# Memory reads of four units as sixteen 32x32 tiles, with new engine orders, in a gated attention and token-mixing kernel

## The chip, the core and the metric

The kernel runs on one core of one Trainium2 chip. The metric is device time in microseconds, the median of several executions. The core has a matmul engine (PE, with its weight loads shown as PEld), a vector engine (DVE), an activation engine (ACT), a general engine (POOL) and a queue engine (SP) that here issues nearly all DMAs. Matmuls write PSUM, which is split into eight banks; a bank holds 512 fp32 values in each of 128 partitions. DVE and ACT read PSUM; everything else lives in SBUF.

## What is computed

The reference mixes two branches with a gate per token (S = 2048 tokens, D = 448):

```python
g = sigmoid((x * gate_w).sum(-1, keepdims=True))
a = A(x, wq, wk, wv, wo, beta)      # attention with a running memory
b = B(x, w1, b1, w2, b2)            # layer norm, then an MLP over the token axis
return g * a + (1 - g) * b
```

Branch A has H = 16 heads of 28 values. The tokens are cut into N = 4 segments of 512. Within a segment the attention is causal softmax attention; from earlier segments a head reads a memory:

```python
phi = lambda t: where(t > 0, t + 1, exp(t))
a_dot = softmax(qs @ ks.T * scale + mask) @ vs      # inside the segment
a_mem = (phi(qs) @ M) / (phi(qs) @ z + 1e-6)        # from earlier segments
o = sigmoid(beta) * a_mem + (1 - sigmoid(beta)) * a_dot
M = M + phi(ks).T @ vs;  z = z + phi(ks).sum(0)
```

The heads' outputs go through `wo`. Branch B is `gelu(h.T @ w1 + b1) @ w2 + b2` on the layer-normed tokens, transposed back; w1 is 2048 x 1792 and w2 is 1792 x 2048.

## The kernel before

**Units and names.** The heads lie in four groups of four, each head padded to 32 rows, so that a group fills 128 partitions. A unit u = 0 to 15 is one segment (u // 4) of one head group (u % 4). `sc{p}_{f}` fills the four score banks 0 to 3 with scores of a pair of units, five fills f for each pair p; ACT's `exp{p}_{f}` empties them (L951) and POOL masks the diagonal blocks (L954). `pv{u}` is the value product (L978), 16 matmuls in four column tiles; each value tile has a 29th column of ones, so the softmax denominator comes with it. `mst{s}` adds a segment's phi(k)v into the memory (L827), and `mstc{s}` (L845) writes it to SBUF as matmul weights. Before, the weights of a group are four 128-column blocks, one per head, each zero outside its head's rows: a 128x128 block-diagonal matrix. `mem{u}` is the memory read of unit u = 4 to 15: one 128x128 matmul on 512 columns of phi(q), into a bank that it takes from the pool of banks 4 to 7. DVE then transposes read and value product out of PSUM (`tm` L992, `ta` L994), adds 1e-6 (`eps` L1003), takes reciprocals (`rec`), scales (`oa`, `om`), adds both (`o`, on POOL or DVE) and transposes back (`ot` L1016). `wo{T}` multiplies token tile T by `wo`, and `ag{T}` applies the gate.

**MLP.** `u{ft}-{st}` are the 14 x 16 matmuls of w1 (448 columns each), followed by the gelu steps `gsq`, `gvh`, `garg`, `gth`, `gelu`. `y{T}-{ft}` are the 16 x 14 matmuls of w2; `fin{T}` (L1082) adds the gated attention and `out{T}` stores the tile. Tile 15 is cut in two parts of 320 and 128 columns; the second carries `#1`.

**Start.** `warm` runs nine matmuls on constants (L625). `dtx{t}_{k}` load x transposed, 512 tokens at a time, in parts of three and one 128-column chunks; `ldx{t}` load four token tiles of x for the layer norm; `ldwv`, `ldwk`, `ldwq` load weights in chunks. `gtr` and `btr` transpose the gate vector and the biases on PE, DVE's `gw`, `b1c`, `b2c` copy them out, and `padk`, `padx`, `padq` (L636) spread the key and query weights into padded heads. Projections are `pra`/`prb` (first chunks), `lo...` (pairs on half the array each, for the last chunk), and `prt` (values), `prk`, `prx`, `prq`. `bns`, `bna` (L885, L887) are the layer norm's statistics and `ln` applies them.

**Order.** Each engine runs a list written out by hand or planner in `ORDER`, in order; a word `name@b` takes PSUM bank b, `name*n` is n consecutive matmuls. Waits follow from the data. In `plan` PE's list is cut into runs between operations on row tiles or half-arrays (modes "r", "h"). Where such a run has a column-tiled operation (mode "c": `pv`, `mst`), all plain matmuls in it (mode "x") are issued as four column tiles too:

```python
for o in self.per_eng["PE"] + [None]:
    if o is None or o.tile != "f":
        for x in run:
            x.cols = x.mode == "x" and any(y.mode == "c" for y in run)
        run = []
```

Of the kernel before, what the change touches and what calls it, by code (L numbers as in the profile page):

```python
# [6 lines left out]
ALU = mybir.AluOpType  # L7
# [7 lines left out]
DH = 28  # L15
# [7 lines left out]
NHG = 4  # L23
# [51 lines left out]
class Sched:  # L75
# [13 lines left out]
    def op(self, eng, fn, reads=(), writes=(), name=None, dma=False, out=False, cost=100.0, prio=0.0, mode="f",  # L89
# [13 lines left out]
        o.tile = mode if mode in "rh" else "f"  # L103
# [196 lines left out]
pv5@5 u10-6*5 sc3_2 u10-11 u11-0@4 u10-12 u11-1 u10-13*3 mst1@5 u11-2*4 sc3_3 lot10@75 u11-6*3 prt11 u11-9 prt10  # L300
# [66 lines left out]
def build_kernel(nc, X, WQ, WK, WV, WO, BETA, W1, B1, W2, B2, GW, OUT):  # L367
# [842 lines left out]
```

## Time and profile before

| | us |
|---|---|
| median of 3 runs | 172.59 |
| lowest, highest | 172.51, 580.05 |
| span of the profiled execution | 170.6 |
| PE busy in it | 166.8 |
| DVE busy | 143.7 |
| ACT busy | 128.0 |
| POOL busy | 61.5 |

The span runs from the first to the last instruction of one execution. Of the three runs two lie within 0.1 us; the third is far off and is not used. Rows of the profile read as: line, engine, operation, tiles, shapes, count, then busy time, mean duration of one in ns, and the idle time just before with what ended it. Matmuls overlap in the pipeline, so the time from one start to the next tells more than a duration. The chain that ended last is followed back from the last instruction to what released each step; its rows are start, duration, engine, line, and how many instructions were merged.

### The profile page before, as it was taken

Reading aid. Unit: us, or ns where it says so; the run is one execution under the profiler, and the core shown is the slowest. Engines: PE = TensorE matmul, PEld = TensorE weight load, DVE = VectorE, ACT = ScalarE, POOL = GpSimd, SP = SyncE. Lnnn points to the kernel's source line nnn. Section 1 sums busy time; section 2 is a strip of 40 time slices with the busy share of each in tenths; the row PEclk is TensorE's granted clock in tenths of the full one; section 3 lists DMA queues with packets and bytes.
Section 4 is the critical chain, followed back from the end, with each engine's and each line's share of the span. In section 5 each row is a group of like instructions: output and inputs, shape, how many; then the busy total and the mean of one; then the engine's idle time right before and its main releaser. Section 6 shows DMA issues by size and latency. Waiting matters only on the chain.

```text
span 170.6 us, 5820 instructions
## 1 busy us (share of the span) xinstructions
PE 166.8 (98%) x2470; PEld 81.3 (48%) x2470; DVE 143.7 (84%) x327; ACT 128.0 (75%) x158; POOL 61.5 (36%) x94
## 2 busy tenths in 40 slices
PE   8899999999999999999999999999999999999994
PEld 2334444455444544545444345444454645555563
DVE  3088998858999899999999989999999999998024
ACT  0359997999999999989999999986897879002100
POOL 5000317255044333229465560446834372500000
DMA  6998994999796816234037286116146251553603
GB/s 145 252 280 274 238 219 138 290 256 183 173 235 168 142 33 184 38 94 138 4 115 207 65 257 112 33 32 187 46 143 200 83 156 50 156 161 112 188 4 108
DMA packets 52589, 25.16 MB, mean 148 GB/s; under 512 B 17092, under 2 KB 52324, under 8 KB 52564
## 3 DMA queue, kind: packets, MB, share of 16 engines
q1 hardware_dynamic: 51772, 24.22, 56.5%
q10 hardware_dynamic: 792, 0.58, 1.7%
q8 instruction: 19, 0.31, 0.8%
q14 instruction: 6, 0.05, 0.1%
HBM read 18.76 MB, written 2.36 MB: 124 GB/s over the span
## 4 chain that ended last, share of the span: by engine, by line
PE 93%; DMA 3%; SPq 2%; DVE 0%; issue 0%
PE t L264 80%; PE t L942 8%; PE t L978 5%; DMA t<-in_A_wk_dram 3%; SPq L521 2%; PE t L827 1%; DVE t L636 0%; DVE t L1082 0%; PE t L860 0%
## 5 line engine op out<-in xcount | busy, mean ns | idle before, releaser
L264 PE MATMUL t<-t 128*32 128x448 bf16 (+6 forms) x1753 | 145.2, 348 | 0.6 <-DMA t<-in_A_wv_dram 0.5
L264 PEld LDWEIGHTS t<-t 128*32 128x32 bf16 (+1 forms) x1753 | 66.8, 97 | 63.3 <-issue 12.8
L951 ACT ACTIVATE t<-t 128x2048 bf16<-128x2048 f32 x40 | 75.1, 1877 | 8.1 <-PE t L942 7.5
L954 POOL TENSOR_SCALAR_AFFINE_SELECT t<-t 128x512 bf16<-128x512 bf16 x64 | 43.4, 694 | 46.4 <-ACT t L951 45.4
L1009 POOL TENSOR_TENSOR t<-t 128x448 bf16<-128x448 f32 x9 | 11.3, 1254 | 18.9 <-DVE t L1007 9.2
L1082 DVE SCALAR_TENSOR_TENSOR t<-t 128x448 bf16<-128x448 f32 (+2 forms) x17 | 10.8, 643 | 8.6 <-PE t L264 8.1
L1036 ACT ACTIVATE t<-t 128x448 bf16<-128x448 f32 x10 | 7.2, 725 | 12.0 <-PE t L264 11.9
L942 PE MATMUL t<-t 28*128 28x512 bf16 (+3 forms) x256 | 15.8, 301 | 0.0
L994 DVE STREAM_TRANSPOSE t<-t 128x512 f32<-128x512 f32 x16 | 11.3, 709 | 1.2 <-PE t L978 0.8
L894 POOL TENSOR_TENSOR t<-t 128x4 f32<-128x4 f32 x4 | 4.3, 1069 | 21.4 <-DVE t L892 16.9
L978 PE MATMUL t<-t 128*32 128x512 bf16 (+3 forms) x256 | 11.5, 299 | 0.0
L942 PEld LDWEIGHTS t<-t 28*128 28x128 bf16 x256 | 4.4, 92 | 14.6 <-ACT t L951 5.9
L1016 DVE STREAM_TRANSPOSE t<-t 128x512 bf16<-128x512 bf16 x16 | 11.0, 689 | 0.1
L885 DVE BATCH_NORM_STATS2 t<-t 128x6 f32<-128x448 bf16 x16 | 9.2, 610 | 0.7 <-DMA t<-in_A_x_dram 0.7
L1060 DVE TENSOR_SCALAR t<-t 128x448 f32<-128x448 f32 x11 | 7.3, 671 | 2.7 <-ACT t L1054 2.7
L1067 DVE SCALAR_TENSOR_TENSOR t<-t 128x448 bf16<-128x448 f32 x14 | 8.7, 622 | 1.0 <-ACT t L1065 1.0
L978 PEld LDWEIGHTS t<-t 128*32 128x32 bf16 x256 | 6.9, 97 | 5.0 <-DVE t L992 0.2
L1054 ACT ACTIVATE t<-t 128x448 f32<-128x448 f32 x14 | 8.9, 636 | 0.3 <-PE t L264 0.2
L1005 DVE SCALAR_TENSOR_TENSOR t<-t 128x448 f32<-128x448 f32 x12 | 9.0, 750 | 0.1
L1062 DVE SCALAR_TENSOR_TENSOR t<-t 128x448 f32<-128x448 f32 x14 | 8.8, 629 | 0.3 <-ACT t L1057 0.2
L750 ACT ACTIVATE t<-t 128x512 bf16<-128x512 bf16 x12 | 7.5, 629 | 1.5 <-DVE t L707 1.5
L992 DVE STREAM_TRANSPOSE t<-t 128x512 f32<-128x512 f32 x12 | 8.4, 704 | 0.2
(71 smaller groups left out, 132.6 us busy)
## 6 DMA issues: line engine op xcount, KB each, us to landing
t<-in_B_w_dram SPq DMA_DIRECT2D x52, 256.0 KB, 3.8
t<-in_A_x_dram SPq DMA_DIRECT2D x4, 448.0 KB, 4.7
out_dram<-t SPq DMA_DIRECT2D x15, 112.0 KB, 2.6
t<-in_B_w_dram SPq DMA_DIRECT2D x8, 128.0 KB, 3.6
t<-in_A_wv_dram ACTq DMA_DIRECT2D x4, 112.0 KB, 4.2
t<-in_A_wo_dram SPq DMA_DIRECT2D x4, 98.0 KB
t<-in_A_wq_dram SPq DMA_DIRECT2D x1, 336.0 KB, 4.8
spare_heads<-t SPq DMA_DIRECT2D x8, 32.0 KB
```

Source lines behind the costliest of these rows:

```text
L264: last = e.matmul(out[q], w[:, q], x, skip_group_check=True, **kw)
L885: op("DVE", lambda e: e.bn_stats(st6[:, t, :], xh[:, t, :]), reads=[R_x[t]], writes=[R_st6[t]], name=f"bns{t}", cost=512, prio=P_PROJ - 10 ...
L942: last = e.matmul(bank(hl)[:, c0 : c0 + w], kT[r, hg, s * 512 + j * 128 : s * 512 + j * 128 + 128], qT[r, hg, s * 512 + 128 * j : s * 512 ...
L951: op("ACT", lambda e: e.activation(pslot(g), ps[:, 0:4, :], ACT.Exp, scale=SCALE), reads=R_bank[0:4], writes=[g.res], take=g, name=f"exp{p ...
L954: op("POOL", lambda e, c0=c0: e.affine_select(pslot(g)[:, :, c0 : c0 + 128], pslot(g)[:, :, c0 : c0 + 128], pattern=[[0, 4], [1, 128]], co ...
L978: last = e.matmul(bank(cb)[32 * hl : 32 * hl + 32, 128 * j : 512], vaug[:, 4 * s + j, 32 * h : 32 * h + 32], pslot(P_fill[u // 2][f])[:, h ...
L994: dv(lambda e: e.transpose(t2[:, 0, :], bank(cb)[:, 0:512]), [bres(cb)], [R_tt[tb][0]], "ta", 630, use=(cb,))
L1005: dv(lambda e: e.scalar_tensor_tensor(n3[0], n3[0], oc, rb[0], op0=ALU.mult, op1=ALU.mult), [R_tt[tb][0], R_rec[tb], R_omcol], [R_tt[tb][0 ...
L1009: op("POOL", lambda e: e.tensor_tensor(o3, n3[0], n3[1], op=ALU.add), reads=R_tt[tb], writes=[R_ob[tb]], name=f"o{u}", cost=1280, port=Tru ...
L1016: dv(lambda e: e.transpose(oT[:, hg, s * 512 : s * 512 + 512], o), [R_ob[tb]], qres(hg, s), "ot", 635)
L1054: op("ACT", lambda e: e.activation(gg[:, q, :], bank(b)[:, 0:D], ACT.Square, bias=b1s[:, ft : ft + 1], scale=math.sqrt(GC)), **buse(b), re ...
L1082: op("DVE", lambda e: e.scalar_tensor_tensor(outst[:, p, c0:c1], bank(b)[:, 0 : c1 - c0], omg[:, T : T + 1], ag(T)[:, c0:c1], op0=ALU.mult ...
```

## The change

**Memory weights.** `mst_sb` keeps 32 columns a head group in place of 128, and `mstc` writes 128x128 in place of 128x512. The mask `maskg` shrinks alike and is made in short steps (`mg0`, `mg1`, `mg2`, `mo0`).

**Reads.** The twelve `mem{u}` become three, `mem1` to `mem3`, one a segment. Each issues sixteen 32x32 matmuls: four heads of four groups, weights and phi(q) from the head's 32 rows. Group hg writes bank hg, which are the score banks 0 to 3, and head hl goes to the 32 partitions at position (hl + hg) % 4. The new mode "q" ends a run in `plan`. Right behind the read come the four `tm` transposes and `eps` steps, into four buffers of their own.

**Turned rows.** The value product `pv` writes its heads at the same turned positions, the mix of 1 - sigmoid(beta) follows (`oc0`), and `wo` is loaded in seven pieces in place of four, so that its rows stand at the turned positions.

**Orders.** All five lists are new.

```diff
-    mst_sb = sb([128, 3, NHG, 128])
+    mst_sb = sb([128, 3, NHG, 32])
...
-    tt = sb([128, 2, 2, 512], F32)
+    tt = sb([128, 6, 512], F32)
...
-        op("DVE", lambda e: e.tensor_tensor(mst_sb[:, s].rearrange("p g (l c) -> p g l c", l=4),
-                                            mst_f32[:, :, None, :].to_broadcast([128, NHG, 4, 32]), maskg[:, :, :, :],
-                                            op=ALU.mult),
+        op("DVE", lambda e: e.tensor_tensor(mst_sb[:, s], mst_f32[:], maskg[:], op=ALU.mult),
...
-        if s > 0:
-            op("PE", lambda e, cols=False: mm(e, bank(mb)[:, 0:512], mst_sb[:, s - 1, hg, :],
-                                              phq[:, hg, (s - 1) * 512 : s * 512], cols, start=True, stop=True),
...
-                    last = e.matmul(bank(cb)[32 * hl : 32 * hl + 32, 128 * j : 512],
+                    last = e.matmul(bank(cb)[32 * ((hl + hg) % 4) : 32 * ((hl + hg) % 4) + 32, 128 * j : 512],
...
+    def mem_four(s):
+        mbs = list(range(NHG))
+        pr = P_ATT + 4 * s
+
+        def fn(e):
+            for hg in range(NHG):
+                for hl in range(4):
+                    r = slice(32 * hl, 32 * hl + 32)
+                    c = 32 * ((hl + hg) % 4)
+                    last = e.matmul(bank(mbs[hg])[c : c + 32, 0:512], mst_sb[r, s - 1, hg, :],
+                                    phq[r, hg, (s - 1) * 512 : s * 512], start=True, stop=True, skip_group_check=True)
+            return last
+
+        op("PE", fn, reads=[R_mst[s - 1]] + [R_phq[hg][s] for hg in range(NHG)], writes=R_bank[0:4],
+           name=f"mem{s}", mode="q", cost=512 / 2.4 + 20, prio=pr)
+        for hg in range(NHG):
+            u, b, t = 4 * s + hg, mbs[hg], tt[:, 2 + hg, :]
+            op("DVE", lambda e, b=b, t=t: e.transpose(t, bank(b)[:, 0:512]), reads=[bres(b)], writes=[R_tt[2 + hg]],
+               name=f"tm{u}", cost=630, prio=pr)
...
+        if u % 4 == 0 and u > 0:
+            mem_four(u // 4)
```

Of the orders, PE's start (two lines of each), the stretch of the first read in the new one, and PE's last words:

```diff
-warm gtr@4 warm2 pra0@5 pra1@6 pra2@7 pra3@4 prb3 prb2 prb0 prb1 lot2 lot0 prt1 prt3 prt2 prt0 pra0_1 pra0_2 pra0_0
-btr@5 lok0_0 lok0_2 prk0_0 prx0_3 prk0_2 prk0_1 loq1_2@74 loq1_0@65 prq1_2h prq1_1 prq1_2 prq1_0 loq0_0 lok1_0@57
+warm warm2 gtr@4 btr@5 pra2@4 pra1@5 pra0@6 pra3@7 prb3 prb0 prb2 pra0_1 pra0_0 prb1 lot2 lok0_0 lot0 prt1 prk0_0
+prk0_1 pra0_2 prt0 prt3 lok0_2 loq0_0 prq0_0 prt2 prq0_1 prk0_2 prx0_3 lok1_2@47 loq1_0@56 prq1_0 prq1_1 prk1_2
...
+u9-6*4 u8-8 loq2_0@75 sc2_2 u8-9*2 u9-10*2 u8-11*2 prq2_1 prq2_0 mem1 u8-13 u9-12 u8-14*2 u9-13*3 u10-0@5*6 pv3@7
+sc2_3 u10-6*2 u11-0@4*7 u10-8*3 sc2_4 loq2_2@67 prq2_2 u10-11*5 prq2_2h u13-0@6*2 sc3_0 u11-7*9 pv4@5 sc3_1 u13-2
...
-y15-0#1@4 y12-12*2 y15-9*5 y15-1#1 y15-2#1 y15-3#1 y15-4#1 y15-5#1 y15-6#1 y15-7#1 y15-8#1 y15-9#1 y15-10#1
-y15-11#1 y15-12#1 y15-13#1""",
...
+y14-1 y15-13 y14-2*5 wo13@7 y13-0@4*6 y14-7*4 y13-6 y14-11*2 y13-7*5 wo12@5 y12-0@7*2 y13-12*2 y12-2*7 y14-13
+y12-9*5""",
```

The DMA queues begin with (first line SP, second ACT, each before and after), and DVE with:

```diff
-dtx0_0 dtx0_1 ldwk0@0 ldwk1 ldwq0@1 ldwqb dtx1_0 dtx1_1 ldx0 ldx4 ldx8 ldbeta ldw1_0_0 dtx2_0 ldx12 dtx2_1 ldw1_0_1
+ldx8 dtx0_0 ldwk0@0 ldwk1 dtx0_1 ldwqb ldwq0@1 ldx4 dtx1_1 dtx1_0 ldx0 ldw1_1_2 ldx12 ldw1_1_0 ldbeta dtx2_1 dtx2_0
...
-ldwv0 ldgw ldwv1 ldwv2 ldwvb ldwkb ldb1 ldb2 cpv2 cpv0 gt0 gt2 cpv1 gt3 gt1 ek0_0 cpk0_3 cpk0_1 cpq1_1 cpq1_2
+ldwkb ldwv0 ldwv2 ldgw ldb2 ldb1 ldwvb ldwv1 cpk0_0 cpk0_1 ek0_0 ek0_1 cpv3 gt3 cpv0 cpv2 gt2 gt1 gt0 cpk0_3 cpk0_2
...
-wo0 ob0 gw padk0 padx0 cpv3 padk1 padx1 padk2 padx2 padq0 padq1 b2c padq2 b1c padq3 cpk0_0 cpk0_2 mk0_0 bns3 bns1
+bns9 padk2 bns11 b2c gw padx2 b1c padx0 padk0 bns8 bna11 bns10 padk1 bna10 padx1 padq3 padq1 padq0 padq2 cpv1 bns4
+bns6 bna6 bns7 mk0_1 bns5 mk0_0 bna8 cpq0_1 cpq0_0 bna9 vpe8 bna5 bns0 bna7 bna0 cpq0_3 bns3 bns2 bns1 bna3 bna1
+cpq1_3 bna2 vpe0 cpq0_2 bns14 nmr0 ln3 bna4 vpe4 bns15 mq1_0 nmr4 phk0_0 bna15 cpk1_1 bns13 bna13 ln0 ln1 ln2 nmr8
```

209 lines of the change are left out of this document (101 added, 108 removed).

## The prediction

> **What bounds the kernel now.** I read the page's first part, then PE's waits, then the chain that ended last (start, us, what).
>
> ```profile
> span 170.6 us, 5820 instructions
> PE 166.8 (98%) x2470; PEld 81.3 (48%) x2470; DVE 143.7 (84%) x327; ACT 128.0 (75%) x158; POOL 61.5 (36%) x94
> PE t L625 <- PEq L1195: 0.8, 1, 0.8
> PE t L264 <- DMA t<-in_A_wv_dram: 0.5, 1, 0.5
> ...
> 3.51 4.99 DMA t<-in_A_wk_dram
> ...
> 9.05 1.47 PE t L264 x6
> ...
> 35.92 0.33 PE t L942 x8
> 36.25 1.63 PE t L264 x32
> 37.88 0.54 PE t L978 x16
> ...
> 57.84 0.49 PE t L827 x64
> ...
> 147.73 20.52 PE t L264 x488
> 168.27 0.35 DVE t L1082
> ```
>
> PE is busy 98%, and the only waits recorded for it are 1.3 us, in the start. From 9.05 us on the chain is PE almost throughout, until one DVE step and a store end the run. So the time is a start, PE's work and an end; what DVE, ACT or POOL save is hidden unless it makes PE wait less.
>
> The chain also holds PE's prices. A value product (x16) is four groups of four column tiles, 512+384+256+128 = 1280 columns, in 0.54 us: 0.42 ns a column, so 0.216 us for 512 columns and 0.189 for 448. A score fill (x8, 0.33 us) streams 512 columns, 0.216, and takes 0.11 more. The 32 matmuls at 36.25 are eight groups of 448 columns, 1.51, and again 0.11 more. Both stand where the next instruction uses the array in another shape (full, column tiles, row tiles, half): 0.11 us is my price for a change of shape.
>
> **PE's work.** Twelve reads of 512 columns go: 12 x 0.216 = 2.59 us. Three packs of sixteen 32x32 tiles come. No row shows row and column tiles in one pack, so it is bounded: 0.216 us if all sixteen stream together, as four do in the value and the score rows; the memory update at 57.84 issues 64 small tiles in 0.49 us, 7.7 ns each, and fifteen of those on top make 0.33. I take 0.216, the nearer row, as four tiles cost nothing extra: 0.65 us, net -1.94. Then the shapes. I counted runs of one shape in both written orders (scores, half-array pairs and the new reads have their own shape; what lies between goes to column tiles if a value product or memory update is in it): 106 before, 111 after (40 score fills and 18 stretches of pairs in both, 29 full ones that become 31, 19 column ones in both, 3 reads): five more changes, +0.5 us. PE has nothing else added, so its work falls by 1.4 us.
>
> **The start.** These rows are the timeline's and the windows' (PE, PEld, DVE, ACT, POOL, clock, DMA share, GB/s), then groups and issues.
>
> ```profile
> 0.82 4.00 PE L625 MATMUL t<-const-bfloat16-1.0 128*128 128x512 bf16 x9 [0.82 <-PEq L1195]
> 1.97 0.93 ACTq L511 DMA_DIRECT2D t<-in_A_wv_dram  x2
> 5.21 1.85 PE L264 MATMUL t<-t 128*128 128x449 bf16 x8
> 9.44 0.80 DVE L636 COPY t<-t 128x392 bf16<-128x392 bf16 x6
> 9.66 1.68 SPq L506 DMA_DIRECT2D t<-in_A_x_dram  x3
> 10.46 3.74 PE L264 MATMUL t<-t 64*128 64x512 bf16 x22
> 13.85 0.63 DVE L885 BATCH_NORM_STATS2 t<-t 128x6 f32<-128x448 bf16 x1 [0.67 <-DMA t<-in_A_x_dram]
> 2.00:3.00 1.00, 1.00 (x4) 0.38 (x3) 0.39 (x1) 0.00 (x0) 0.94 (x4) 1.00 1.01 245
> 13.00:14.00 1.00, 1.00 (x8) 0.61 (x7) 0.33 (x2) 0.76 (x2) 0.00 (x0) 1.00 1.08 372
> t<-in_A_x_dram SPq DMA_DIRECT2D x4, 448.0 KB, 4.7
> t<-in_B_b_dram ACTq DMA_DIRECT2D x1, 4.0 KB, 4.2
> ```
>
> A good mark is lok0_0, the first product that needs all padded key weights: at 10.46 now. The new order moves lot0, prt0 to prt3 and pra0_2 behind it: 5 x 449 + 1024 columns, 1.4 us, and two changes of shape, so 1.6 us less lies ahead of it. Behind it PE then has 0.2 us *more* than before, the saving of 1.4 included: the gain is kept only if lok0_0 starts earlier.
>
> It has to pass three things. First, SP's first issue is now ldx8, 448 KB. The DMA engines are full from 2 us on (share 1.01, 1.08), so its 0.459 MB at 372 GB/s push all behind it back by 1.23 us. The key weights ldwk0, landed at 3.51 + 4.99 = 8.50 so far, overtake dtx0_1 (131 KB at 245 GB/s, 0.54), so they land near 9.2. Second, DVE has two statistics (2 x 0.63) and two small sums in its queue among the key pads; with four pads at the 0.13 us of the six at 9.44 that is 2.0 us: lok0_0 at 11.2. If the load hides in time the queue doesn't use, the weights land at 8.50 and it is 10.5. Third, btr now stands ahead of all value products on PE, and gw follows bns9, padk2, bns11 and b2c on DVE. ldb1 is ACT's sixth issue; at 0.47 us each it goes out near 3.6 and, with 4.2 to landing, frees btr near 7.8 and pra2 near 8.3, against 5.21. Eight value products of 449 columns, two key products of 1024 and the pair lot2 then lie ahead of lok0_0, 2.7 us: 11.0. I take 11.0, between the ends 10.2 (all a little quicker) and 12.0 (two of them adding up): 0.54 late plus the 0.2 makes **+0.7 us (-0.1 to +1.7)**.
>
> The moves behind lok0_0 have to be covered. ldx0 goes out behind ldx8 and ldx4 now, so it lands 2 x 1.23 after the 13.85 that bns0 waited for, at 16.3. DVE's queue holds the copies cpq0_3 and cpq1_3 behind bns0, and these free score and projection banks that PE takes again with loq0_2 and lok1_0. Counting PE's columns from lok0_0 at 11.0 puts lok1_0 near 20.9; bns0 and three more statistics (0.63), four short sums (0.13, as the pads) and two 512-wide copies (0.68, as L845's step below) put the end of cpq1_3 near 20.7. That is about even; it costs nothing while DVE has no more to make up, and up to 0.5 us, inside the bound above, if it has. Three more ldwo issues hold SP for 3 x 0.56 (the x loads took 1.68 for three) and wait there for wo0, which DVE now clears only after the layer norm; w1 blocks queue behind them. No wait of PE above is for a w1 block, so they land ahead of their use now; I put nothing on it, and at most the same 1.7 us if that lead is gone.
>
> [...] The warm-up matmuls run 0.42 us apart for 512 columns against 0.216 later, though the clock column says 1.00 throughout. [...] The half pace of the start agrees with the 0.42; a fall back to it no row here shows. Priced from the rows alone it is a rival below.
>
> **The three stops.** A read now writes all four score banks, and the next score fill waits until DVE has transposed each out.
>
> ```profile
> 60.00:70.00 10.00, 10.00 (x143) 4.85 (x139) 9.50 (x20) 9.97 (x12) 3.14 (x5) 1.00 0.29 83
> 90.00:100.00 10.00, 10.00 (x109) 4.15 (x102) 10.00 (x22) 9.78 (x11) 5.79 (x7) 1.00 0.51 150
> L992 DVE STREAM_TRANSPOSE t<-t 128x512 f32<-128x512 f32 x12 | 8.4, 704 | 0.2
> L752 DVE TENSOR_SCALAR t<-t 128x512 bf16<-128x512 bf16 x12 | 3.5, 293 | 0.3 <-ACT t L750 0.3
> L845 DVE TENSOR_TENSOR t<-t 128x512 bf16<-128x512 f32 x3 | 2.0, 681 | 0.0
> L840 DVE COPY t<-t 128x128 f32<-128x128 f32 x1 | 0.3, 282 | 0.0
> L1011 DVE TENSOR_TENSOR t<-t 128x448 bf16<-128x448 f32 x3 | 1.8, 614 | 0.0
> ```
>
> Four transposes and the one small step written among them (mq, mk or eps) take 4 x 0.70 + 0.29 = 3.1 us. Behind the reads PE has filler until sc2_3, sc4_3 and sc6_3: for mem1 thirteen u products and pv3, 3.1 us; for mem2 and mem3, by the same column price, 3.0 and 2.9. So they fit by nothing to spare, if DVE is ready when the read ends. PE waits for sc in order: mm1 and mm2 products queue behind it, and ACT's next exp too. I put 0.1 us on each, **+0.3 (0 to 3)**, 3 being DVE a microsecond late each time: it is 95 to 100% busy there. Its own work eases by 3 x (0.68 - 0.28), mstc now being a quarter as wide (0.28 is msta's size); two sums, o9 and o14, come over from POOL, 2 x 0.61, and undo it, and of the copies and scalings that ACT and DVE trade, DVE has one more. mg0 shrinks from 128x448 to 128x16, with a few short steps behind it, and the turned rows of pv and wo change no count on PE: nothing, under PE's work, unless they add to DVE's lateness.
>
> **The end.** The last tile was the 128-column part of tile 15; now it is y12, 448 columns.
>
> ```profile
> L1082 DVE SCALAR_TENSOR_TENSOR t<-t 128x448 bf16<-128x448 f32 (+2 forms) x17 | 10.8, 643 | 8.6 <-PE t L264 8.1 <-DMA out_dram<-t 0.5
> out_dram<-t SPq DMA_DIRECT2D x15, 112.0 KB, 2.6
> out_dram<-t SPq DMA_DIRECT2D x1, 80.0 KB, 1.6
> out_dram<-t SPq DMA_DIRECT2D x1, 32.0 KB, 1.5
> ```
>
> fin12 takes 0.64 instead of 0.35: +0.29. Its store is 112 KB: 2.6 in the median of busy stretches, 1.6 for the 80 KB of the same end, against 1.5. Nothing else is stored then, so I take 1.8. **+0.6 (0.4 to 1.4).**
>
> **Sum.** 0.7 + 0.3 + 0.6 = +1.6 on the span of 170.6: 172.2. The median lies 2.0 above that span (172.59), and so the forecast is 174.2.
>
> **Rivals.**
> - *The reads stall the scores.* DVE reaches the first transpose late, and each stop holds PE by as much. Point of decision: 0.7 us late per stop in place of 0.1 makes 176.0, 2% over before. For: no spare in the three sums, DVE full. Against: PE waits for no engine now, with DVE as full. At 1.3 late each: 174.2 + 3.6 = 177.8. Chance 0.16.
> - *A start at half rate.* lok0_0 at 12.0 and the clock of the warm-up again for a stretch as long as that (4.0 us, half of it lost): +1.0 + 2.0, 177.2. [...] Chance 0.09.
> - *The tiles of a pack don't run together.* Four row tiles write each bank. If they go one by one, 3 x 0.216 more per read, 176.1 in all; all sixteen in turn, 3 x 15 x 0.216 = 9.7, 183.9. For: no row has it. Against: the turn by group puts the four into different partitions. Chance 0.05. [...]
> - *The gain is kept.* lok0_0 near 10, no stop, a quiet last store: 172.59 - 0.1 + 0.4 = 172.9 by my lower bounds; 171.2 if start and end are as before. Chance 0.17, of which 0.03 faster by over 2%, which would also need the start's waits to go.
>
> **Numbers.** 0.53 for the forecast (172.9 to 175.8 by itself). 2% is 3.45 us, about what a measurement of this kernel can tell from no change: 169.1 and 176.0. Slower by more: 0.16 + 0.08 of the half-rate start + 0.04 of the tiles = 0.28. Faster by more: 0.03. Within: 0.69. The range, 171.4 to 177.8, leaves out the best of the last rival and the worst of the others.
>
> **What would show it.** Right: three groups of sixteen 32x32 matmuls near 0.22 us apart from their change of shape; lok0_0 near 11.0; no PE wait over 0.3 us behind a read; PE's last matmul near 169.3 and the end 0.6 later after it. Wrong: PE waits for the transposes of L992's successor or for exps in the middle, a pack over 0.4 us, or first value products before 6 us with lok0_0 before 10.

## The result and the profile after

| | before | after |
|---|---|---|
| median, us | 172.59 (172.51 to 173.04) | 189.83 (188.87 to 191.07) |
| ratio, 95% interval | | 1.10 (1.0947 to 1.1052) |
| span of the profiled execution | 170.6 | 188.2 |

Of the four executions of the kernel before, the one at 580.05 us is left out, and times here and below are medians of the executions in the faster of two states of the chip. The kernel became 10% slower, by 17.2 us; forecast was 174.2 with 171.4 to 177.8. First the part of the page with busy times, and its chain that ended last, of the kernel after:

```profile
span 188.2 us, 5657 instructions
PE 170.0 (90%) x2389; PEld 79.8 (42%) x2395; DVE 155.1 (82%) x332; ACT 129.6 (69%) x157; POOL 63.4 (34%) x92
DVE 44%; PE 27%; DMA 9%; ACT 8%; POOL 4%; SPq 3%; issue 2%; ACTq 0%; DVEq 0%; POOLq 0%
```

The same chain line of the kernel before:

```profile
PE 93%; DMA 3%; SPq 2%; DVE 0%; issue 0%
```

PE fell from 98% to 90% of the span, and the chain that sets the end now runs mostly through DVE. DVE is busy 11.4 us longer, although what it has to compute is nearly the same. PE's longest waits after (who waited for whom, us, times, longest):

```profile
PE t L808 <- DMA t<-in_gate_w_dram: 2.2, 1, 2.2
PE t L972 <- DVE t L763: 2.2, 1, 2.2
PE t L264 <- DMA t<-in_B_w_dram: 1.7, 1, 1.7
PE t L972 <- DVE t L1074: 1.1, 2, 0.8
PE t L264 <- DVE t L901: 0.9, 1, 0.9
```

No single wait explains 17 us. To place the loss I set each matmul's start in the trace, plus the PE work still to come by the prediction's own prices (0.42 ns a column, 0.11 us a change of shape), against PE's whole work: the excess is what PE has lost up to there. "Start" is the loss up to the first MLP product `u0-0`, "middle" the loss from there to the last matmul.

| kernel | start | middle | DVE busy | span |
|---|---|---|---|---|
| before | 4.1 | 0.6 | 143.7 | 170.6 |
| after | 9.0 | 14.0 | 155.1 | 188.2 |

So the +17.6 on the span is +4.9 in the start, +13.4 in the middle, +0.8 behind the last matmul and -1.4 of PE work (the prediction's own figure, as the prices are). The start differs from execution to execution: in the kernel after and five of the runs below whose start is the same (e3, e6, e9, e10, e13), `u0-0` begins between 29.8 and 31.1 us, so the start's loss lies between 7.7 and 9.0, and the profiled execution of the kernel after is the latest of the six. A difference of 1 us in that column says nothing. From the last score fill, at 162.22, to the last matmul, PE lost only 0.4 in 22 us of work: the prices hold for the new kernel as well.

**Where DVE's 11 us come from.** Timeline rows of the kernel after around 66 us (start, us, engine, line, operation), DVE first, then POOL:

```profile
66.13 0.72 DVE L750 TENSOR_SCALAR t<-t 128x512 bf16<-128x512 bf16 x1
66.77 1.11 DVE L752 SCALAR_TENSOR_TENSOR t<-t 128x512 bf16<-128x512 bf16 x1
67.81 0.67 DVE L1074 TENSOR_SCALAR t<-t 128x448 f32<-128x448 f32 x1
68.51 0.62 DVE L1076 SCALAR_TENSOR_TENSOR t<-t 128x448 f32<-128x448 f32 x1
69.06 1.05 DVE L1005 SCALAR_TENSOR_TENSOR t<-t 128x448 bf16<-128x448 f32 x1
70.03 0.70 DVE L986 STREAM_TRANSPOSE t<-t 128x512 f32<-128x512 f32 x1
65.80 1.54 POOL L954 TENSOR_SCALAR_AFFINE_SELECT t<-t 128x512 bf16<-128x512 bf16 x2
68.81 1.80 POOL L954 TENSOR_SCALAR_AFFINE_SELECT t<-t 128x512 bf16<-128x512 bf16 x2 [1.47 <-ACT t L951]
```

The same two steps of phi(k) in the kernel before, at about the same time, with the pair of masks over before them:

```profile
68.19 0.29 DVE L752 TENSOR_SCALAR t<-t 128x512 bf16<-128x512 bf16 x1
68.52 0.69 DVE L754 SCALAR_TENSOR_TENSOR t<-t 128x512 bf16<-128x512 bf16 x1
65.83 1.34 POOL L954 TENSOR_SCALAR_AFFINE_SELECT t<-t 128x512 bf16<-128x512 bf16 x2 [1.67 <-ACT t L951]
```

Before, the masks run from 65.83 to 67.17 and the two DVE steps come behind them. After, both steps lie beside a pair of masks (65.80 to 67.34) and take 0.72 for 0.29 and 1.11 for 0.69; the scaling at 69.06 takes 1.05 beside the next pair. The transpose, which reads PSUM, stays at 0.70. Sorted over the whole trace after: of the twelve phi(q) products (L777), the six that touch no POOL work take 678 ns on average, the six that do 1116; phi(k)'s (L752) 679 and 1083; the transposes `ta` out of PSUM 704 and 711. The steps that are stretched read and write SBUF, but not all such steps are: the transposes `ot`, from SBUF to SBUF with one input, take 700 and 704. Stretched on average are steps with two SBUF inputs (besides phi's the scaling L1005, 674 alone and 1053 beside POOL work, and L1076, 609 and 834; L1081, with 595 and 647, hardly) and tensor-scalar steps from SBUF (phi's L750, 280 and 583, and L774, 272 and 620); tensor-scalar steps out of PSUM are not (L1074, 662 and 673). The two stretched kinds overlap POOL's work for about 38 us after, less than 19 before; in the old order more of POOL's work lies beside transposes (22 us, 14 of it out of PSUM; 12 and 8 after). The group rows show it as means (kernel after, then before; busy us, mean ns):

```profile
L777 DVE SCALAR_TENSOR_TENSOR t<-t 128x512 bf16<-128x512 bf16 x12 | 10.8, 897 | 0.1
L752 DVE SCALAR_TENSOR_TENSOR t<-t 128x512 bf16<-128x512 bf16 x12 | 9.8, 814 | 0.1
L954 POOL TENSOR_SCALAR_AFFINE_SELECT t<-t 128x512 bf16<-128x512 bf16 x64 | 47.6, 753 | 63.9 <-ACT t L951 62.3
```

```profile
L779 DVE SCALAR_TENSOR_TENSOR t<-t 128x512 bf16<-128x512 bf16 x12 | 8.4, 705 | 0.0
L754 DVE SCALAR_TENSOR_TENSOR t<-t 128x512 bf16<-128x512 bf16 x12 | 8.3, 691 | 0.1
L954 POOL TENSOR_SCALAR_AFFINE_SELECT t<-t 128x512 bf16<-128x512 bf16 x64 | 43.4, 694 | 46.4 <-ACT t L951 45.4
```

The masks take longer too, 753 ns against 694. Why steps and masks hold each other up no trace here shows, only with which steps it comes: phi's steps with two inputs are stretched by some 0.4 us on average, a good part of a mask's 0.75, and the transposes, with one input, are not.

### The profile page after: what moved, and what is told of

Same layout as the page of the kernel before. It is cut to its first block, busy times and chain, and to the rows that moved or that the text cites. A ratio compares the mean times of both kernels' runs of the same rounds, so it can differ in the third digit from the quotient of the medians.

```text
span 188.2 us, 5657 instructions
## 1 busy us (share of the span) xinstructions
PE 170.0 (90%) x2389; PEld 79.8 (42%) x2395; DVE 155.1 (82%) x332; ACT 129.6 (69%) x157; POOL 63.4 (34%) x92
## 4 chain that ended last, share of the span: by engine, by line
DVE 44%; PE 27%; DMA 9%; ACT 8%; POOL 4%; SPq 3%; issue 2%; ACTq 0%; DVEq 0%; POOLq 0%
PE t L264 23%; ACT t L951 4%; DVE t L777 4%; DVE t L752 4%; DVE t L1076 4%; DVE t L901 3%; DVE t L885 3%; DVE t L1074 3%; DVE t L1026 3%; DMA t<-in_B_b_dram 3%; DMA t<-t 2%; DMA t<-in_B_w_dram 2%; DVE t L1081 2%; PE t L972 2%; DVE t L750 2%
## 5 line engine op out<-in xcount | busy, mean ns | idle before, releaser
L264 PE MATMUL t<-t 128*32 128x448 bf16 (+10 forms) x1624 | 144.0, 348 | 6.2 <-DMA t<-in_B_w_dram 1.7
L264 PEld LDWEIGHTS t<-t 128*32 128x32 bf16 (+2 forms) x1630 | 65.2, 97 | 70.8 <-issue 16.8
L954 POOL TENSOR_SCALAR_AFFINE_SELECT t<-t 128x512 bf16<-128x512 bf16 x64 | 47.6, 753 | 63.9 <-ACT t L951 62.3
L1050 ACT ACTIVATE t<-t 128x448 bf16<-128x448 f32 x9 | 6.5, 723 | 15.3 <-PE t L264 15.3
L986 DVE STREAM_TRANSPOSE t<-t 128x512 f32<-128x512 f32 x16 | 11.3, 706 | 3.1 <-PE t L972 3.0
L1000 POOL TENSOR_TENSOR t<-t 128x448 bf16<-128x448 f32 x7 | 9.5, 1354 | 11.6 <-DVE t L998 7.8
L703 ACT ACTIVATE t<-t 128x512 bf16<-128x512 f32 x11 | 6.5, 598 | 9.8 <-PE t L264 9.5
L1007 DVE STREAM_TRANSPOSE t<-t 128x512 bf16<-128x512 bf16 x16 | 11.2, 702 | 0.1
L777 DVE SCALAR_TENSOR_TENSOR t<-t 128x512 bf16<-128x512 bf16 x12 | 10.8, 897 | 0.1
L942 PEld LDWEIGHTS t<-t 28*128 28x128 bf16 x256 | 4.4, 92 | 14.6 <-ACT t L951 7.3
L1076 DVE SCALAR_TENSOR_TENSOR t<-t 128x448 f32<-128x448 f32 x14 | 10.1, 722 | 0.3
L752 DVE SCALAR_TENSOR_TENSOR t<-t 128x512 bf16<-128x512 bf16 x12 | 9.8, 814 | 0.1
L772 ACT ACTIVATE t<-t 128x512 bf16<-128x512 bf16 x12 | 7.6, 630 | 3.2 <-DVE t L763 2.2
L748 ACT ACTIVATE t<-t 128x512 bf16<-128x512 bf16 x12 | 7.5, 636 | 2.6 <-DMA t<-t 2.6
(75 smaller groups left out, 142.6 us busy)
```

The source lines that it names most:

```text
L264: last = e.matmul(out[q], w[:, q], x, skip_group_check=True, **kw)
L752: op("DVE", lambda e: e.scalar_tensor_tensor(kphi[:, p, :], ks, 0.0, kphi[:, p, :], op0=ALU.max, op1=ALU.add), reads=kres(hg, tc) + [R_kph ...
L777: op("DVE", lambda e: e.scalar_tensor_tensor(ph, qs, 0.0, ph, op0=ALU.max, op1=ALU.add), reads=qres(hg, tc) + [R_phq[hg][tc]], writes=[R_p ...
L942: last = e.matmul(bank(hl)[:, c0 : c0 + w], kT[r, hg, s * 512 + j * 128 : s * 512 + j * 128 + 128], qT[r, hg, s * 512 + 128 * j : s * 512 ...
L954: op("POOL", lambda e, c0=c0: e.affine_select(pslot(g)[:, :, c0 : c0 + 128], pslot(g)[:, :, c0 : c0 + 128], pattern=[[0, 4], [1, 128]], co ...
L986: dv(lambda e: e.transpose(tt[:, ia, :], bank(cb)[:, 0:512]), [bres(cb)], [R_tt[ia]], "ta", 630, use=(cb,))
```

## Experiments

Theories at the outset: (1) the start is late and the rest follows from it; (2) the new order makes DVE collide with POOL's masks; later (3) DVE simply has too much work in the middle, and (4) the reads hold the score banks too long. The table gives all runs but e8, e11 and e12, which stand in the text; ratios are against the kernel before on the same chip. Start, middle and DVE busy come from one profiled execution of each run. Code is shortened to the changed words.

| run | time | ratio (95%) | start | middle | DVE busy |
|---|---|---|---|---|---|
| e1 start in order | 189.14 | 1.0958 (1.085, 1.1065) | 8.0 | 14.6 | 154.6 |
| e2 longer warm-up | 189.83 | 1.0997 (1.0921, 1.1074) | 6.6 | 16.3 | 154.9 |
| e3 narrow masks | 181.68 | 1.0525 (1.0378, 1.0673) | 8.2 | 5.5 | 142.6 |
| e4 before, `ldx8` first | 177.89 | 1.0306 (1.0232, 1.038) | 9.3 | 0.6 | 143.9 |
| e5 less statistics | 189.29 | 1.0963 (1.0925, 1.1) | 8.9 | 13.0 | 148.1 |
| e6 no reads | 191.87 | 1.1112 (1.1049, 1.1176) | 8.2 | 17.3 | 153.9 |
| e7 before, narrow masks | 172.56 | 0.9997 (0.9982, 1.0012) | 4.0 | 1.2 | 139.7 |
| e9 narrow masks, POOL work kept | 185.93 | 1.0774 (1.0685, 1.0863) | 7.7 | 10.2 | 154.0 |
| e10 SP order | 188.41 | 1.0889 (1.0837, 1.094) | 8.7 | 12.7 | 155.4 |
| e13 half transposes | 188.49 | 1.0933 (1.0891, 1.0976) | 7.8 | 13.0 | 147.4 |
| e14 e1, e3, e10, e13 together | 179.26 | 1.0397 (1.0356, 1.0438) | 8.0 | 3.6 | 137.1 |
| e15 the same and e5 | 176.65 | 1.0249 (1.013, 1.0369) | 6.0 | 4.7 | 131.4 |
| e16 e1 and e5 | 187.35 | 1.0871 (1.082, 1.0922) | 5.4 | 14.9 | 148.0 |
| e17 before, POOL's mask work doubled | 189.36 | 1.0972 (1.0951, 1.0994) | 4.0 | 17.5 | 161.6 |
| e18 e1 and e10 | 187.73 | 1.0871 (1.0824, 1.0917) | 8.0 | 11.8 | 155.5 |

### Is it the late start?

e1 put the start in order: `ldx8` behind the first weights on SP, the gate vector and biases right behind the first value weights on ACT's queue, and on DVE the copies and pads ahead of the statistics.

```diff
-ldx8 dtx0_0 ldwk0@0 ldwk1 dtx0_1 ldwqb ldwq0@1 ldx4
+dtx0_0 ldwk0@0 ldwk1 dtx0_1 ldwqb ldwq0@1 ldx8 ldx4
...
-ldwkb ldwv0 ldwv2 ldgw ldb2 ldb1 ldwvb ldwv1 cpk0_0
+ldwv0 ldgw ldb2 ldb1 ldwv1 ldwv2 ldwvb ldwkb cpk0_0
...
-bns9 padk2 bns11 b2c gw padx2 b1c padx0 padk0 bns8 bna11 bns10 padk1 bna10 padx1 padq3 padq1 padq0 padq2
+b2c gw b1c padk0 padx0 padk1 padx1 padk2 padx2 padq3 padq1 padq0 padq2 bns9 bns11 bna11 bns8 bns10 bna10
```

> The changed kernel with its start put in order: ldx8 behind the query weights, the gate vector and the biases right behind the first value weights, and in DVE's list the copies and pads ahead of the first layer-norm statistics. Theory 1 (late start, then drift: the new orders fit a start some 3 us earlier, and the PE waits in the middle come from DVE and POOL steps that fall together since): first value product near 6 us, lok0_0 near 10.5 in place of 13.6, PE waits behind lok0_0 under 5 us in place of 13.5, time 173 to 178. Theory 2 (the new orders or the new reads lose the time in the middle whatever the start): only the start comes back, time 186 to 187.

The first padded key product `lok0_0` came at 10.7 instead of 13.6 (12.3 to 13.6 in the six executions with the same start), but the time fell by 0.7 only, which is inside the intervals; neither theory's time was met. At `u0-0` e1 stands at 30.0, no earlier than the others' 29.8 to 31.1: the gain was gone there already. On the way PE waited 1.5 us for copies on DVE (L719), for which it doesn't wait in the kernel after, and its longest waits behind it (2.2 us for L763, 2.1 for a part of w1) are for the same steps as in the kernel after.

e2 added 14 warm-up matmuls to close PE's idle stretch:

> The changed kernel with 14 more warm-up matmuls, so that PE does not idle while it waits for the gate vector; nothing else. If the 0.37 us between the first value products is the half clock: they go 0.19 us apart, lok0_0 near 11.5 in place of 13.6, and the time falls by 2 us or, if the later waits shrink with it (theory 1), by 3 to 8. If the products wait for data: the spacing and the time stay.

PE's longest wait in the kernel after, at `gtr`, as the timeline has it, and the window from 8 to 13 us (width, then busy time and instructions of PE, PEld, DVE, ACT, POOL, clock, DMA share, GB/s):

```profile
7.47 0.19 PE L808 MATMUL t<-t 128*128 128x3 bf16 x1 [2.22 <-DMA t<-in_gate_w_dram]
8.00:13.00 5.00, 4.56 (x13) 1.80 (x13) 3.14 (x16) 0.00 (x0) 0.00 (x0) 1.00 1.16 339
```

The same window in e2:

```profile
8.00:13.00 5.00, 4.51 (x25) 1.97 (x25) 3.98 (x18) 0.68 (x2) 0.00 (x0) 1.00 1.17 335
```

In the same busy time e2 ran 25 matmuls where the kernel after ran 13. Behind its idle stretch of 2.2 us the kernel after ran at half pace until about 13 us (starts 0.37 us apart instead of 0.19). The clock column shows 1.00 in both. `lok0_0` came at 13.6 there and at 11.2 in e2, so half pace cost 2.4 us; against the other five executions, where it ended sooner (from 11.0 us on), 1.1 to 2.1. Giving it back changed nothing that shows at the end (189.83, give or take 1.3).

That the idle stretch is what brings half pace isn't shown. These are e1 and e16 (below; the same start but for less work on DVE) from 6.5 to 9 us, with the same columns as above:

```profile
6.50:9.00 2.50, 2.50 (x7) 0.97 (x8) 0.51 (x4) 0.00 (x0) 0.00 (x0) 1.00 1.10 243
6.50:9.00 2.50, 2.41 (x12) 0.97 (x10) 0.72 (x4) 0.00 (x0) 0.00 (x0) 1.00 1.13 216
```

e1 ran 7 matmuls at half pace, e16 12 at full, although PE's longest wait in the start was 0.5 us in e1 and 0.7 in e16 (0.8 in both before the first matmul). In e1 and in the kernel after the warm-up itself ran at half pace to its end (512-column matmuls 0.43 us apart in the kernel after, six in 2.77 us in e1), so PE may never have left it there. In executions of one start half pace ended at different times (11.0 to 13.0 us); what brings it on and what ends it no run here shows.

e4 asked whether the old order is as fragile. It is the kernel before with `ldx8` as SP's first load:

> The kernel before with ldx8 issued first on SP; nothing else. If a late load costs what it moves and no more: lok0_0 1.2 us later, time 173.5 to 174.2. If such a list of orders falls apart with a small delay: over 176.

```profile
9.06 5.14 PE L264 MATMUL t<-t 128*128 128x449 bf16 x15 [3.10 <-DMA t<-in_A_x_dram]
8.00:13.00 5.00, 3.94 (x12) 1.17 (x12) 0.47 (x2) 0.00 (x0) 0.00 (x0) 0.50 1.10 289
```

One load moved cost 5.2 us of start: PE waited 3.1 us for x, and half pace came too, here with the clock column at 0.50. But all of it stayed in the start: the middle lost 0.6 as before. The old middle takes a late start as it is; the new one has a loss of its own. A late start explains at most the start's own +4.9.

### The masks

e3 cuts the masks to 2 of 128 columns, which leaves out nearly all of the masks' effect on the scores:

```diff
-e.affine_select(pslot(g)[:, :, c0 : c0 + 128], pslot(g)[:, :, c0 : c0 + 128], pattern=[[0, 4], [1, 128]],
+e.affine_select(pslot(g)[:, :, c0 : c0 + 2], pslot(g)[:, :, c0 : c0 + 2], pattern=[[0, 4], [1, 2]],
```

> The changed kernel with each causal mask on POOL over 2 columns in place of 128 (the mask is left out but for those). If POOL's masks stretch the DVE steps that run beside them: phi steps of q beside POOL near 0.68 us in place of 1.1, DVE busy near 145 in place of 155, PE waits behind lok0_0 well under 13.5 us, time 176 to 182. If the DVE steps are long for another reason or PE's waits come from the order (theory 2): DVE stays near 155 or the time over 186.

e7 makes the same cut in the kernel before:

> The kernel before, with GpSimd's causal masks over 2 columns instead of 128 (the masks' effect on the scores is left out): the control to the same cut in the kernel after, which gave 8 us. If the masks cost the kernel after because VectorE had become its bound, they cost the kernel before next to nothing: VectorE's busy time falls from 143.7 to about 140, but TensorE binds, and the time is 170.5 to 172.5. If masks cost every order alike (a general cost of GpSimd's port use), it falls by 5 us or more.

The page of e3, and its group rows:

```profile
span 178.9 us, 5657 instructions
PE 167.6 (94%) x2389; PEld 80.1 (45%) x2395; DVE 142.6 (80%) x332; ACT 129.0 (72%) x157; POOL 34.1 (19%) x92
PE 35%; DVE 31%; DMA 15%; ACT 8%; SPq 4%; POOL 3%; issue 2%; ACTq 0%; DVEq 0%; POOLq 0%
L777 DVE SCALAR_TENSOR_TENSOR t<-t 128x512 bf16<-128x512 bf16 x12 | 8.5, 705 | 0.1
L954 POOL TENSOR_SCALAR_AFFINE_SELECT t<-t 128x8 bf16<-128x8 bf16 x64 | 18.7, 300 | 82.2 <-ACT t L951 80.6
```

phi(q)'s mean is back at 705 ns, DVE's busy time is 12.5 lower and the time 8 us. In the old order the same cut gives nothing (0.9997): there the masks hold up nothing that PE waits for. But narrow masks also have the probabilities ready 0.45 us sooner. e9 splits the two: narrow masks, and behind each a second POOL instruction of the old size on a tile of its own.

```diff
+op("POOL", lambda e: e.affine_select(other[:], other[:], pattern=[[0, 4], [1, 128]], ...
+   reads=[R_oth], writes=[R_oth], name=f"oth{p}_{f}_{j}", ...
```

> The kernel after with the causal masks over 2 columns (their effect on the scores left out), and behind each mask a second GpSimd instruction of the old mask's size on an SBUF tile that nobody else uses. What the narrow masks alone gave (181.7) can have two reasons. If it is GpSimd's claim on SBUF beside VectorE's steps, the second instruction brings it back: VectorE's busy time returns to about 155 (142.6 with narrow masks alone) and the time to 187 to 191. If it is that the probabilities are ready 0.6 us sooner after each exp, nobody waits for the second instruction: the time stays at 181 to 183 with VectorE at about 143.

```profile
PE 168.8 (92%) x2395; PEld 79.6 (43%) x2395; DVE 154.0 (84%) x332; ACT 130.0 (71%) x157; POOL 79.4 (43%) x157
L966 POOL TENSOR_SCALAR_AFFINE_SELECT t<-t 128x512 bf16<-128x512 bf16 x64 | 46.4, 725 | 0.0
```

DVE's busy time is back (154.0), as the first expectation had it, but only about half of the time: ratios 1.0525, 1.0774, 1.10 for narrow masks, POOL work kept, masks whole. The steps between them are 4.3 us (give or take 3) for the second instructions and 3.9 (give or take 2) for the wait for the masks themselves. So both play a part, and the halves are rough; the second instructions also stand in POOL's queue ahead of the next mask, so the 4.3 need not be DVE's stretch alone.

e17 turns it round: the kernel before, whole, with the same second instruction behind each mask.

> The kernel before, whole, with a second GpSimd instruction of a mask's size on an unused SBUF tile behind each mask. If any order is slowed where GpSimd and VectorE claim SBUF together, VectorE's busy time goes from 143.7 to above 150 and the time up by 5 us or more (178 or later). If the old order has the slack for it, VectorE grows as much and the time stays within 2 us of 172.6, as TensorE still binds.

```profile
PE 170.9 (91%) x2463; PEld 79.7 (43%) x2470; DVE 161.6 (86%) x327; ACT 128.8 (69%) x158; POOL 112.7 (60%) x159
L787 DVE SCALAR_TENSOR_TENSOR t<-t 128x512 bf16<-128x512 bf16 x12 | 9.1, 767 | 0.0
PE t L989 <- POOL t L962: 3.9, 4, 1.6
PE t L264 <- DVE t L1005: 2.2, 3, 1.5
```

The old order goes from 172.6 to 189.4, the kernel after's time, with no change in TensorE's work: more work on POOL alone can cost that much. It is not all DVE's stretch: POOL is now busy 60%, and the value products wait 3.9 us for masks that queue behind the second instructions. The first of the two expectations held: the old order has no slack for this. With its own masks alone DVE does lose time, 4.0 us of busy time by e7, but none of it reaches the end.

### Is it the amount of DVE's work, or the reads?

e5 takes the layer norm's statistics over 64 of 448 columns (the rest left out), e6 leaves the reads out and lets their transposes read an SBUF tile:

```diff
-e.bn_stats(st6[:, t, :], xh[:, t, :])
+e.bn_stats(st6[:, t, :], xh[:, t, 0:64])
```

```diff
-e.transpose(t, bank(b)[:, 0:512])
+e.transpose(t, flat)
```

> The kernel after, with the layer norm's statistics taken over the first 64 of the 448 columns (the rest of the columns are left out of mean and variance): it sheds about 16 x 0.4 us of VectorE work, nearly all of it in the first 40 us. Theory A (VectorE comes late out of the layer norm, and because it is late its SBUF steps fall beside GpSimd's masks): with some 6 us less ahead of them the steps move out from under the masks; VectorE's busy time falls by clearly more than the work shed (below 145 us against 155.1), and the time falls to 180 or less. Theory B (the new lists themselves put these steps where the masks run, whatever the lateness): the stretch stays, busy time falls by 6 to 7 us (about 148), and the time by no more than the 6 us shed, 183.5 to 188.

> The kernel after, with the three reads left out of TensorE (no 32x32 tiles, nothing written into the four score banks) and their twelve VectorE transposes reading an SBUF tile of the same size instead: the output leaves out the memory term. If holding four score banks at once from the read to the last transpose is what costs the middle its time, the time falls by 5 us or more (below 185). If VectorE's stretch beside the masks is the cause, the same VectorE work stays and the time falls by 3 us or less (187 to 190), about the three reads' own 1.1 us and the 2 us in which neighbours waited for them.

e5 shed 7.0 us of DVE, as theory B had it, and won 0.5 in time, which is inside the intervals; DVE's lateness out of the layer norm is not what makes it collide. e6 was no faster (DVE busy 153.9), so the reads and their hold of four score banks are not the cause (theory 4 falls).

e11 sheds DVE work in the middle, the 28 transposes out of PSUM over half their columns:

```diff
-e.transpose(tt[:, ia, :], bank(cb)[:, 0:512])
+e.transpose(tt[:, ia, 0:256], bank(cb)[:, 0:256])
```

> The kernel after with the 28 VectorE transposes of the attention's outputs and of the reads (ta, tm) over 256 of 512 columns: half of each stays stale, the rest of the work is as before. They read PSUM and were not stretched by GpSimd; this sheds about 28 x 0.35 = 9.5 us of VectorE work, all of it between 58 and 175 us. If VectorE's load in the middle is the bound, the time falls by 6 to 10 us (180 to 184). If it is the round trips (VectorE to SP's transposes and gathers and back), with VectorE only part of them, it falls by 2 to 4. If VectorE is not the bound, by less than 1.5.

It took 192.82, ratio 1.1147 (1.1084 to 1.121). But the memset that fills the stale halves stood right ahead of the first masks and cost 2.5 us beside the layer norm. e13 has it in POOL's idle time:

> As e11 (the 28 transposes ta and tm over 256 of 512 columns, half of each stale), with the memset of the stale tiles moved to GpSimd's idle time before 20 us. e11 lost 2.5 us more than the kernel after by the scores of the first pair and, from the next pair on, exactly as much as it. If VectorE's amount of work does not bind the middle, this repeats: 188.5 to 190.5. If it does and e11 was only shifted, the time falls by 4 us or more (below 186).

```profile
PE 169.6 (91%) x2389; PEld 79.8 (43%) x2395; DVE 147.4 (79%) x332; ACT 129.3 (69%) x157; POOL 65.0 (35%) x93
```

7.7 us less DVE work, 1.3 us less time, and the intervals overlap. The middle loses 13.0 instead of 14.0. So the amount of DVE's work alone is not the bound either (theory 3): what DVE saves turns into DVE waiting. My reading, which no run isolates: a step beside a mask is late where another engine waits for it, while most of the work saved here was not on that path.

### The path itself

Rows of the chain of the kernel after, from 65 us to the next segment's DMA transpose (start, us, engine and line):

```profile
65.24 0.97 DVE t L1076
66.21 0.64 DVE t L750
66.85 1.03 DVE t L752
67.88 0.03 DVE t L1074
67.91 4.09 DMA t<-t
...
72.03 0.63 ACT t L748
72.66 1.77 ACT t L951
74.43 0.14 issue
74.56 0.52 PE t L1018 x16
...
75.11 1.31 DVE t L1026 x2
...
83.42 1.05 DVE t L1005
...
86.48 1.22 SPq L755
```

It goes through phi(k) on DVE, its DMA transpose, ACT's exponential for the next phi(k) (which waits for the buffer), an exp, the read that waits for the score banks, DVE's transposes, and, behind a full DVE queue, the next DMA transpose at 86.48. The loads behind that on SP come late; PE waits for one at 92.96:

```profile
92.96 0.36 PE L264 MATMUL t<-t 128*128 128x448 bf16 x1 [1.68 <-DMA t<-in_B_w_dram]
```

e10 moves those loads ahead of the transposes:

```diff
-ldw1_6_0 tk2_1 ldw1_6_1 gq2_2 gq2_3 ldw2_0_1 tk1_2 gq2_1 ldwo1b ldw1_6_3 ldw2_2_0
+ldw1_6_0 ldw1_6_1 ldw1_6_3 ldw2_0_1 ldwo1b tk2_1 gq2_2 gq2_3 tk1_2 gq2_1 ldw2_2_0
```

> The kernel after with four loads (the second and fourth part of W1's last block, the second of W2's first, one piece of wo) moved ahead of the DMA transpose of segment 2's phi(k), which waits on SP for a late VectorE step, 12 us in the kernel after. If SP's order costs what the trace shows at unit 13 of the first MLP product (PE waits 1.84 us for the load), that wait goes and the time falls by 1.5 to 2 (about 188). If VectorE's lateness sets the middle and the wait is only where it shows, the next wait behind it grows by as much and the time stays within 0.7 of 189.8.

That wait went, and the time fell by 1.4. That is just at the edge of the intervals. e18 adds e1's start to it, with no work left out:

> The kernel after, whole, with the start in order (189.1 alone against 189.8) and the four loads ahead on SP (188.4 alone). If the two gains add, 187.5 to 188; if the wait at SP was only moved, 188.5 to 189.5. Neither reaches the kernel before.

It took 187.73: the medians add as expected, but e18's interval overlaps e10's, so that e1's part is a gain at all isn't shown. The kernel remains 8.7% slower than before.

### All cuts together

> The kernel after with both cuts: the start's loads and VectorE's first steps put in an order that gives back 3 us at the first scores, and GpSimd's masks over 2 columns (their effect on the scores left out). If the two causes stand side by side, the start's 3 us come through once VectorE no longer binds: 176 to 179, with 6 us or less lost in the middle. If the middle is bound by VectorE for another reason too, the start's gain is lost again: 181 to 182.5, as with the narrow masks alone.

e8's time is that of one execution, 180.65, between its two expectations, and so has no interval.

> The kernel after with all the cuts at once: the start in order, the narrow masks, the four loads ahead on SP, the half transposes (masks' effect and half of each transpose left out). If start, VectorE's load in the middle and SP's order are the whole of what the change lost, TensorE binds again and the time comes near the model's 161.9 + 6.5 to 8 at the start + 3.3 behind the last matmul + 2 around the span: 174 to 177. If something else in the new lists holds TensorE up, it stays above 178.

e12 gave 179.75, ratio 1.0404 (1.0349, 1.046), so by its second branch something else in the new lists still held TensorE up; it also carries e11's misplaced memset. e14 mends that:

> As e12 (start in order, narrow masks, four loads ahead on SP, half transposes; masks' effect and half of each transpose left out) with the same memset moved. e12 lost 2.0 us between the first product of the MLP and the second pair of scores, where the narrow masks alone lost nothing; that goes: 177.5 to 179. Of its loss over the kernel before the start would then be nearly all.

e15 adds e5's cut, and e16 has only the cuts to the start:

> As e14, with the layer norm's statistics over 64 of 448 columns besides. If the start is held at 30 us by two limits, the late first products on PE and the layer norm's chain on VectorE, both are lifted now: the first product of the MLP starts at 27.5 to 28.5 (30.1 to 31.1 in the kernel after and in e1, e8 and e12), and as nothing in the middle binds, the time is 174.5 to 176.5. If a third limit holds the start, it starts at 29.5 or later and the time stays at 177.5 to 179.

> The kernel after with the start in order and the layer norm's statistics over 64 of 448 columns (the rest left out of mean and variance); masks, SP's order and the rest of VectorE's work whole. The first product of the MLP starts about 2.5 us sooner than in the kernel after (28.5 against 31.1). If the middle loses time by its own order, whatever time it starts at, the 2.5 us reach the end: 186.5 to 188. If the middle runs to a clock of its own (what binds there began before the first product and is not moved by it), they are lost again: 189 to 190.5.

With masks, SP and transposes cut, e14's middle loses 3.6 us and its start 8.0, where the kernel before loses 0.6 and 4.1. So about 3 us of what e14 is slower stay in the middle, and not nearly all is the start, as I had expected. The start has two limits, one just behind the other: with both lifted `u0-0` starts at 28.1 (e15) and 27.5 (e16), with one alone at 30.0 (e1) and 30.9 (e5), no earlier than without either (29.8 to 31.1). e16's start is 2.3 to 3.6 us earlier and its time 2.5 shorter, while its DVE also does 7 us less. e15 is unclear: its two executions, 175.52 and 177.78, lie on both sides of the 176.5 that I had as the upper end, and its interval reaches from 1.3% to 3.7% over the kernel before.

## Why the prediction was wrong

**PE's work: right, as far as it shows.** The -1.4 is counted and not measured, but with its prices PE loses only 0.6 us in the whole middle of the kernel before and 0.4 in the last 22 us of the new one. The pack behaves as priced: in the row at 74.56 in the fence below, sixteen matmuls, then the next instruction 0.37 us after their start; predicted were 0.22 and a change of shape of 0.11. Behind the other two packs PE waits for another engine (0.16 and 0.65 us), so their length can't be read here; in e14 all three take 0.37. The rival that tiles run one by one did not come.

```profile
74.56 0.44 PE L1018 MATMUL t<-t 32*32 32x512 bf16 x16 [0.52 <-ACT t L951]
74.93 2.64 PE L264 MATMUL t<-t 128*32 128x448 bf16 x52
```

**The start: right mechanism, too small.** `btr` was expected at 7.8 (8.0) and `pra2` at 8.3 (8.6). But I put `lok0_0` at 11.0 and it came at 13.6. Half pace, a rival to which I gave 0.09, accounts for 2.4 of these 2.6 in that execution (e2), and for 1.1 to 2.1 in others. The 0.09 was my estimate; what brings half pace on no run shows. PE's idle stretch comes from a row that I had not followed: `gtr` stands ahead of all projections, and the gate vector landed at 7.5. In the table's terms the start was to lose 2.1 more than before (0.5 late, 1.6 of work moved behind it); it lost 3.6 to 4.9 more. Close behind lies the layer norm's chain on DVE, which I had found "about even" at `lok1_0`: by `u0-0` it had taken back all that e1 gained.

**The end: right**, +0.8 against +0.6.

**The three stops: direction right, place wrong.** Expected +0.3, at most 3; PE's waits next to the three reads add up to some 2 to 3. That is the bound I named, but it is not where the middle went, as e6 shows.

**The step that failed** is in "What bounds the kernel now": that what DVE, ACT or POOL do is hidden unless it makes PE wait less, so that the new lists of DVE and POOL could be counted by instructions alone, with +0.3 us (0 to 3) for what DVE's lateness costs PE. The runs showed +13.4 in the middle in its place. I counted two sums moved, one copy more, some narrower steps, and put the durations of the old trace on them. Those durations are not properties of the steps. They hold only while a step does not meet a mask (phi's steps: 0.68 us alone, 1.08 and 1.12 on average beside POOL's work), and the old order keeps them apart more often. DVE grew by 11.4 us, nearly all in steps whose list had not changed. The first rival had "DVE reaches the transposes late", but bounded it at three places and at 1.3 us each; the lateness was everywhere. With narrow masks the middle's loss falls from 14.0 to 5.5 (e3).

**What the 17.2 us are.** Shown: about 8 are the masks (e3), roughly half of them POOL's work as such and not the wait for the masks (e9). 1.4 are SP's order (e10), at the edge of the intervals. +0.8 is the end, and -1.4 PE's work. What the start's +3.6 to +4.9 are worth at the end is open: e2 gave back at least 1.1 us of the start, yet its time stayed (give or take 1.3); e16 gave back 2.3 to 3.6 (with less DVE work) and 2.5 came through. What e14 still loses in the middle, 3.6, lies mainly where `mem1` waits for an exp and at one score fill; that stayed open too. The causes overlap, and the parts need not add up exactly. Not shown: that the new lists, rearranged by hand so that DVE's SBUF steps avoid the masks with all the work kept, would reach the kernel before. No such order was tried. Nor is it known why the new order came to place them so.

## What to carry to other kernels

A duration from a trace can belong to its neighbours in time: phi's 512-element steps took 0.68 us alone here and 1.08 and 1.12 on average beside POOL's work. Before moving DVE or GpSimd steps in a full order, mark which of them read SBUF and which read PSUM, and see what runs beside them now; put beside GpSimd work what this trace shows unstretched, PSUM steps and transposes (`ta` 0.70 and 0.71 us), and keep steps with two SBUF inputs away from it. Such an order was not tried here; what the runs show is that with narrow masks 8 us came back (e3), roughly half of them from the wait for the masks (e9). And PE at 98% with DVE at 84% did not mean slack on the others here (172.6 to 189.4 in e17): test it by adding instructions on an SBUF tile that nobody else uses, as in e17, before rearranging anything.

## What the runs showed of the hardware

- 512-element steps on DVE with two SBUF inputs took 0.68 us alone, and beside POOL's work 1.12 (phi(q), six cases, 0.68 to 1.63) and 1.08 (phi(k), four cases); phi(k)'s tensor-scalar step of 0.28 took 0.58 (four cases). Transposes out of PSUM (`ta`, 0.70 and 0.71) did not change, nor did transposes from SBUF to SBUF (`ot`, 0.70 and 0.70).
- PE ran at half pace (449-column matmuls 0.37 us apart, not 0.19) while the granted clock read 1.00: in the kernel after from 8.6 to 13 us behind an idle stretch of 2.2 us, and in e1 until 9.8 us with no wait over 0.54 us since the warm-up. In e4, behind a wait of 3.1 us, the clock read 0.50.
- With the same start, half pace ended between 11.0 and 13.0 us in six executions of six kernels, and `u0-0` began between 29.8 and 31.1.
- Sixteen 32x32 matmuls that write four banks, four row tiles into each at different partitions, all started within 54 ns in the kernel after, and the next instruction followed 0.37 us after the first where PE did not wait.
- One 448 KB load moved to the head of the queue cost 5.2 us at the start (e4); from queue time alone I had put 1.2.
